# The temperature-threshold set-up ahead of the constants, and two places for the tail copies, in a fused attention and mixture-of-experts kernel

## The chip, the cores and the metric

The kernel runs on one core of a Trainium2 chip. Times are microseconds (us) of the device. A run of the program is one execution; three executions of the kernel before are timed, and one more was taken with the profiler, which gives the trace.

## The reference

The program computes attention with a threshold, and passes its result, token by token, to a mixture of experts with one chosen expert per token:

```python
scores = scale * np.matmul(q, k.transpose(0, 1, 3, 2))      # 4 batches, 8 heads, 576 x 576, head size 64
thresh = np.max(scores, axis=-1, keepdims=True) - tau
scores = np.where(scores >= thresh, scores, -1e9)
attn = softmax(scores); attn_out = attn @ v
x = attn_out.transpose(0, 2, 1, 3).reshape(2304, 512)
expert = argmax(x @ w_gate)                                  # 8 experts, 576 rows of capacity each
out[i] = gate_w[i] * (relu(x[i] @ w1[expert]) @ w2[expert])  # 512 -> 1024 -> 512
```

Everything is in 32-bit floating point; `tau` is one number that arrives in memory as an input.

## The kernel before, in words

**Staging.** The 32 (batch, head) combinations are worked as 16 pairs `s` of two heads; four pairs make a batch (`s` = 4b + a, a = 0 to 3). Per pair the kernel loads k, q and v; splits q and k into a high and a low 16-bit part ("hi" on ScalarE, `emit_hi` L767; "lo" on VectorE for the first two pairs and on GpSimd for the others, `emit_lo` L775); turns both so that the head size lies on partitions (`kT`, `qT`); makes the scores `s` on TensorE and their row maxima on VectorE (`emit_max`); works out each row's threshold (`emit_m`), which is added to q as two more columns and turned again ("tm"); makes the scores a second time, transposed and with the threshold in them (`d`); takes the exponential on ScalarE and masks on VectorE (`emit_keep` L940); splits the probabilities into two 16-bit parts; multiplies by v into the bank `xo` (`emit_av`); copies `xo` to `xs` on ScalarE (`emit_xe` L982), sums and inverts the denominators on VectorE (`emit_r`), and scales on GpSimd into the token rows `xr` (`emit_xm` L994).

**Tails.** 576 rows are four blocks of 128 and a tail of 64. The part x = 2 of a pair is the tail of both heads: 64 partitions, 2 x 64 columns. Pairs a = 0, 1 put it on partitions 0 to 63, pairs a = 2, 3 on partitions 64 to 127, in the tile `xrt`, which holds one batch's tails. All 16 pairs use one tile `xs2` for the copy and one for the reciprocals.

**The first pair** is turned differently: on TensorE, by a matmul with the identity (`emit_pturn` L804: k high, k low, then q), and copied out by VectorE and ScalarE (`emit_pturned` L809, `emit_hi_rows` L816). In the text below, hik0 and lok0 are the high and low part of k of pair 0, likewise hiq0, hik1 and so on; ptk0, ptk1 and ptq0 are the three matmul turns; pck0 and pck1 copy the turned k (VectorE and ScalarE), pcq0 and pcq1 the turned q (VectorE and ScalarE); vs0 and vh0 scale and round v of pair 0, vs1 that of pair 1. tq1, tk1 are the turns of pair 1, done by DMA from the SyncE queue. The score matmuls of pair 0 read kT and qT, so they need all four copies.

**Set-up.** Before the pairs VectorE fills constants (L264 to L293), clears the pad columns of `kn`, `qn`, `xs` (L732 to L740), and only then, in program order, does `emit_tau` (L295): the two numbers `g` (tau's sign, times 64) and `ntau`, from `tau_t`. `g` is the scale that hiq0 and hiq1 multiply with.

**The planner.** The order of everything after the set-up is worked out when the program is built, by a list scheduler (class `Plan`). Each piece of work is a task with an engine, a planned duration, tasks that it must follow, and a priority (lower goes first). Going forward in planned time, the planner gives an engine the task of lowest priority number among those that could start within 90 ns of the first one that could (`WINDOW`). For a task that follows a load, the earliest start is the planned end of the transfer plus `LAND[kind]`; all tasks that follow work on an engine get some 150 to 230 ns for the hand-over. The result is one fixed order per engine; on the chip each engine takes its instructions in that order, and a wait of the one at the head holds all that follow. The planner's times are nowhere on the chip; they only set the order.

The loads go out on SyncE (k0, then q1, then k1), ScalarE (q0) and GpSimd (v0, v1). After the pairs come the experts' matmuls (from about 333 us), whose code is the same before and after.

Of the kernel before, what the change touches and what calls it, by code (L numbers as in the profile page):

```python
# [10 lines left out]
F32 = mybir.dt.float32  # L11
# [4 lines left out]
ALU = mybir.AluOpType  # L16
# [4 lines left out]
P = 128  # L21
QK_SCALE = 64.0
# [4 lines left out]
MC = 4096.0  # L27
# [7 lines left out]
class Plan:  # L35
# [155 lines left out]
def attention_moe_kernel(ctx: ExitStack, tc: tile.TileContext, q, k, v, tau, w_gate, w1, w2, cap, out):  # L191
    nc = tc.nc
    B, H, S, D = q.shape
    NTOK, DM = out.shape
    E, _, F = w1.shape
    NJ = S // P
    TAIL = S - NJ * P
# [15 lines left out]
    const = ctx.enter_context(tc.tile_pool(name="const", bufs=1))  # L213
# [12 lines left out]
    V = nc.vector  # L226
# [11 lines left out]
    cum = const_of("cum", [E], F16)  # L238
# [45 lines left out]
    V.tensor_scalar(out=half[:, 0:1], in0=tok_l, scalar1=float(HP), scalar2=None, op0=ALU.is_ge)
    V.tensor_copy(out=hslot[:, 0:2], in_=hs_i)
    V.scalar_tensor_tensor(
        out=half[:, 1:2], in0=half[:, 0:1], scalar=-float(HP), in1=tok_l, op0=ALU.mult, op1=ALU.add
    )
    for t in (slice(0, NF), slice(NL, SLOTS)):
        V.tensor_scalar(out=hslot[:, 0, t], in0=hslot[:, 0, t], scalar1=half[:, 0:1], scalar2=None, op0=ALU.add)  # L290
    V.tensor_scalar(
        out=hslot[:, 2], in0=hslot[:, 0], scalar1=float(HP), scalar2=half[:, 1:2], op0=ALU.mult, op1=ALU.add
    )  # L293

# [374 lines left out]
    if True:  # L669
# [324 lines left out]
        def emit_xm(s, x):  # L994
            t, _, r1, rows, n = xs_of(s, x)
            b, a, _ = heads_of(s)
            if b not in xrows:
                xrows[b] = [xp.tile([P, NJ, ROW], F32, name="xr", tag="xr"), None]
            if x == 2 and xrows[b][1] is None:
                xrows[b][1] = xp1.tile([P, 1, HD], F32, name="xrt", tag="xrt")  # L1000
            if x < 2:
                h = 2 * a + x
                out = xrows[b][0][:, :, h * D + h // HH:h * D + h // HH + D]
            else:
                out = xrows[b][1][rows, 0, a % 2 * P:(a % 2 + 1) * P].rearrange("p (x d) -> p x d", d=D)
            nc.gpsimd.tensor_tensor(out=out, in0=t[:, :, 0:D], in1=r1.to_broadcast([P if x < 2 else TAIL, n, D]), op=ALU.mult)

# [217 lines left out]

        T("xd0", "S", 1150, first_row, [("s", 1, 4)], 20, dma=20, kind="rows")
        plan.fill = lambda *_: 0
        T(("ltau",), "S", 475, lambda: nc.sync.dma_start(out=tau_t, in_=tau.partition_broadcast(P)), [], -60, dma=60, kind="load")
# [5 lines left out]
        T(("lwg",), "S", 475, lambda: nc.sync.dma_start(out=wg[:, :, 0:E], in_=w_gate.rearrange("(c p) e -> p c e", p=P)), [("s", 1, 2)], 20, dma=230, kind="load")  # L1234

# [6 lines left out]
        for s in range(NPR):  # L1242
# [3 lines left out]
            for is_q in (False, True):  # L1246
                n = "q" if is_q else "k"
                src, raws = (q, qraws) if is_q else (k, kraws)
                eng, en, occ = (nc.scalar, "A", 460) if (s, is_q) in FIRST_A else (nc.sync, "S", 600)
                T(("l" + n, s), en, 3 * occ, partial(load, src, raws[s % NRAW], s, eng), last("lo" + n, s - NRAW) + ([("tk", 0), ("tq", 0)] if s == 2 else [("tk", 2), ("tq", 2)] if s == 3 else []), u + PR["ld"] + is_q, dma=(728, 90, 90), kind="load")  # L1250
                nat = s - (NQN if is_q else NKN)
# [11 lines left out]
                if s == 0:  # L1263
# [12 lines left out]
                    continue  # L1276
                T(("t" + n, s), "S", 0, partial(emit_turn_q if is_q else emit_turn_k, s), [("lo" + n, s)] + users + ([("tm", 0)] if s == 2 else []), u + PR["tk"] + is_q, dma=2016, kind="turn")
            vfree = last("av", s - NV, 2, 0) + last("av", s - NV, 1, NJ - 1)
# [43 lines left out]
            for x in range(3):  # L1322
# [298 lines left out]
```

## Time and profile before

| | us |
|---|---|
| three timed executions | 615.66, 617.41, 619.67 |
| their median | 617.41 |
| the profiled execution | 614.46 |
| its span, first to last instruction | 612.4 |
| time of the profiled execution outside the span | 2.06 |
| mean granted clock of TensorE | 0.967 of full speed |

Engines are named PE (TensorE), PEld (its weight loads), DVE (VectorE), ACT (ScalarE), POOL (GpSimd), SP (SyncE); a "q" behind the name is the engine's sequencer or its DMA queue. A start in a view is counted from the first instruction of the span. The stretch up to 16 us is the set-up with pair 0's turns; the score matmuls of pair 0 begin at about 14 to 15 us; attention ends at about 345 us.

### The profile page before, as it was taken

What the parts mean: (1) busy time and instruction counts of PE and PEld (TensorE: products, weight loads), DVE (VectorE), ACT (ScalarE), POOL (GpSimd) and SP (SyncE); (2) the same over time, 40 slices, a digit from 0 to 9 for tenths busy, and PEclk for the clock granted to TensorE, in tenths of its full rate; (3) what the DMA queues carried; (4) which work ended last, traced back from release to release, by engine and by line L of the source; (5) the groups of instructions that cost most, each with busy time, mean ns of one, the idle gap of its engine ahead of it and who ended that gap; (6) DMA issues with size and microseconds to landing.
All of it is one profiled execution on the core that took longest, in us unless ns stands there. A gap on an engine that the chain in (4) does not pass through costs nothing.

```text
span 612.4 us, 16304 instructions
## 1 busy us (share of the span) xinstructions
PE 529.5 (86%) x6122; PEld 343.0 (56%) x6122; DVE 433.5 (71%) x999; ACT 396.5 (65%) x551; POOL 446.6 (73%) x382
## 2 busy tenths in 40 slices
PE   2868889887998979997687868699999999999993
PEld 1334545554664646665466744575774687468651
DVE  5886787889897899887776895355555555555652
ACT  5585887897897869896378755356676547625400
POOL 5365967878997689897499446308998868956864
PEclk9897999999999999998798988899999999999997
DMA  6967775578777686872152868754497529643952
GB/s 142 167 123 152 137 155 106 130 105 190 123 151 138 103 205 117 139 106 70 60 155 91 294 190 256 201 65 138 172 232 201 167 84 266 193 169 78 209 179 102
DMA packets 165327, 92.80 MB, mean 152 GB/s; under 512 B 141172, under 2 KB 153528, under 8 KB 165243
## 3 DMA queue, kind: packets, MB, share of 16 engines
q1 hardware_dynamic: 152458, 49.59, 43.0%
q0 software_dynamic: 12352, 41.80, 21.1%
q8 instruction: 53, 0.87, 0.6%
q10 hardware_dynamic: 432, 0.30, 0.2%
q14 instruction: 32, 0.25, 0.1%
HBM read 53.25 MB, written 10.24 MB: 104 GB/s over the span
## 4 chain that ended last, share of the span: by engine, by line
PE 61%; DVE 13%; DMA 11%; ACT 6%; POOL 4%; issue 3%; another core or an unknown queue 1%; SPq 0%; POOLq 0%; ACTq 0%; DVEq 0%
PE b L406 12%; PE s L846 7%; DMA qT<-qn 6%; PE d L846 6%; PE b L399 6%; PE gp L445 6%; PE xo L445 6%; PE xo L958 6%; PE b L445 5%; DVE mx L873 3%; PE xo L970 3%; DMA out_dram<-latey,oix 2%; DVE w2b L942 2%; DVE w1b L942 2%; POOL p L912 2%
## 5 line engine op out<-in xcount | busy, mean ns | idle before, releaser
L873 DVE TENSOR_REDUCE mx<-s 128x1 f32<-128x512 f32 x144 | 95.4, 680 | 26.6 <-PE s L846 25.9
L846 PE MATMUL s<-kT,qT 128*128 128x512 f16 (+2 forms) x576 | 95.8, 306 | 21.1 <-DMA qT<-qn 8.3
L846 PE MATMUL d<-qT,kT 128*128 128x512 f16 (+2 forms) x576 | 88.5, 305 | 10.4 <-DVE w1b L942 4.2
L406 PE MATMUL b<-w1b,latex 128*128 (+2 forms) x816 | 80.7, 276 | 6.9 <-ACT latex L376 3.2
L331 ACT ACTIVATE ws<-ws 128x1024 f32<-128x1024 f32 x48 | 50.5, 1051 | 47.7 <-DMA ws<-in_moe_w_dram 47.7
L406 PEld LDWEIGHTS <-latex 128*128 128x128 f16 (+1 forms) x816 | 63.1, 103 | 23.2 <-issue 6.5
L942 DVE SCALAR_TENSOR_TENSOR w2b<-d,ntau,w2b 128x1024 f32<-128x1024 f32 x56 | 71.4, 1275 | 5.0 <-ACT w2b L938 4.7
L334 POOL TENSOR_TENSOR w1b<-ws,w1b 128x1024 f16<-128x1024 f32 x24 | 51.2, 2142 | 29.8 <-ACT w1b L332 29.6
L912 POOL TENSOR_TENSOR p<-w2b,p 128x1024 f16<-128x1024 f32 x33 | 70.5, 2144 | 2.6 <-DMA qr<-in_q_dram 1.5
L334 POOL TENSOR_TENSOR w2b<-ws,w2b 128x1024 f16<-128x1024 f32 x24 | 51.0, 2137 | 20.5 <-ACT w2b L332 20.3
L938 ACT ACTIVATE w2b<-d 128x1024 f32<-128x1024 f32 x56 | 57.1, 1019 | 12.5 <-PE d L846 12.2
L846 PEld LDWEIGHTS <-qT 128*128 128x128 f16 (+1 forms) x640 | 34.9, 102 | 53.7 <-issue 25.4
L846 PEld LDWEIGHTS <-kT 128*128 128x128 f16 (+1 forms) x640 | 36.6, 101 | 49.9 <-issue 31.1
L445 PEld LDWEIGHTS <-lateh 128*128 128x128 f16 (+1 forms) x408 | 30.7, 103 | 33.8 <-issue 0.8
L958 PEld LDWEIGHTS <-p 128*128 128x128 f16 x1056 | 41.9, 99 | 11.3 <-POOL p L912 1.8
L399 PEld LDWEIGHTS <-w1b 128*128 128x128 f16 x768 | 43.9, 98 | 6.9 <-issue 5.4
L399 PE MATMUL b<-earlyx,w1b 128*128 128x128 f16 x768 | 47.1, 219 | 0.0
L958 PE MATMUL xo<-vH,p 128*128 128x65 f16 x704 | 45.2, 196 | 1.7 <-POOL p L912 1.7
L958 PE MATMUL xo<-vL,p 128*128 128x64 f16 x352 | 41.9, 193 | 0.4 <-issue 0.4
L332 ACT ACTIVATE w2b<-ws 128x1024 f16<-128x1024 f32 x24 | 25.4, 1057 | 21.2 <-PE gp L445 20.6
L318 POOL DMA_DIRECT2D ws<-in_moe_w_dram x50 | 37.4, 751 | 1.2 <-POOL w2b L334 0.9
L908 ACT ACTIVATE p<-w2b 128x1024 f16<-128x1024 f32 x33 | 34.7, 1056 | 0.4 <-DVE w2b L942 0.4
(250 smaller groups left out, 1228.6 us busy)
## 6 DMA issues: line engine op xcount, KB each, us to landing
ws<-in_moe_w_dram POOLq DMA_DIRECT2D x50, 512.0 KB
ws<-in_moe_w_dram SPq DMA_DIRECT2D x14, 512.0 KB
kr<-in_k_dram SPq DMA_DIRECT2D x16, 256.0 KB
qr<-in_q_dram SPq DMA_DIRECT2D x15, 256.0 KB
v<-in_v_dram SPq DMA_DIRECT2D x28, 128.0 KB
kr<-in_k_dram SPq DMA_DIRECT2D x32, 16.0 KB
v<-in_v_dram POOLq DMA_DIRECT2D x4, 128.0 KB
qr<-in_q_dram SPq DMA_DIRECT2D x30, 16.0 KB
```

Source lines behind the costliest of these rows:

```text
L318: eng.dma_start(out=t, in_=src)
L331: nc.scalar.activation(out=t, in_=t, func=AF.Copy, scale=W_SCALE)
L334: nc.gpsimd.tensor_tensor(out=dst[:, :, 1, :], in0=t, in1=dst[:, :, 0, :], op=ALU.subtract)
L399: nc.tensor.matmul(out=hp[:, f * P:(f + 1) * P], lhsT=wb[0][:, o:o + P], rhs=xT[t][:, xi], start=(d == 0 and z == 0), stop=(d == NB - 1 an ...
L406: nc.tensor.matmul(out=hp[m, 0:FC], lhsT=xT[t][:, xi, m], rhs=wb[0][:, bass.ds(r + (2 * d + wi) * FC, FC)], start=(d == 0 and z == 0), sto ...
L445: nc.tensor.matmul(out=yp[m], lhsT=h[:, o, hi, m], rhs=wb[1][:, bass.ds(r + wi * DM, DM)], start=(z == 0), stop=(z == len(ops) - 1),)
L846: nc.tensor.matmul(out=out, lhsT=l, rhs=r, start=(z == 0), stop=(z == 1), **kw)
L873: V.tensor_reduce(out=m[:, i, 0:1], in_=ps_s[i % 2], axis=AX.X, op=ALU.max)
L912: eng.tensor_tensor(out=p[:, 1], in0=x, in1=p[:, 0], op=ALU.subtract)
L938: nc.scalar.activation(out=t, in_=d, func=AF.Exp, scale=sc_s)
L942: V.scalar_tensor_tensor(out=t, in0=d, scalar=ntau, in1=t, op0=ALU.is_ge, op1=ALU.mult)
L958: nc.tensor.matmul(out=ps_x[:, j * DV:j * DV + r.shape[-1]], lhsT=l, rhs=r, start=(z == 0), stop=(z == len(ops) - 1))
```

## The change

Three things are done.

1. `emit_tau` stands ahead of most of the set-up. On VectorE there remain before it `ones`, `ident16`, the pads of buffer 0 (`pads(0)`) and one memset of `qT`. The rest are tasks of the plan that follow tau on VectorE: `("pad", 1)` (planned 800 ns, priority -59), `("pad", 2)` (400 ns, -30), `("const", 0)` (1500 ns, -12) and `("const", 1)` (1000 ns, -11). Users of these constants get the tasks as predecessors.
2. The planner's landing times: tau's goes from 560 to 2100 ns (kind "tau"), that of k0 and q0 from 560 to 2300 ns (kind "load0"). All other loads, q1 and k1 among them, keep 560.
3. The tail copy has two tiles, `xs2` and `xs3` (by a % 2), of two blocks instead of four, and `emit_xe` of a tail follows the scaling of two pairs back, not of the pair before. In pairs a = 2, 3 the scaling of the tail runs over all 128 partitions: the 64 of this pair and again the 64 of pair a - 2, which lie in the same tile.

```diff
-    LAND = {"load": 560, "turn": 960, "rows": 2000, "move": 1030, "gather": 980}
+    LAND = {"load": 560, "tau": 2100, "load0": 2300, "turn": 960, "rows": 2000, "move": 1030, "gather": 980}
...
     V.memset(ones, 1.0)
-    V.memset(cum, 0.0)
-    V.memset(wg, 0.0)
-    V.memset(zero, 0.0)
...
+    def more_consts(i):
+        if i == 0:
+            V.memset(cum, 0.0)
+            V.memset(wg, 0.0)
+            V.memset(zero, 0.0)
+            for i in range(2):
+                V.tensor_copy(out=tri2[:, i * HP:(i + 1) * HP], in_=tri[:, 0:HP])
...
+            return
+        V.tensor_copy(out=hslot[:, 0:2], in_=hs_i)
...
-        xss = [right.tile([P, NJ, D + 2], F32, name=f"xs{i}") for i in range(3)]
-        rcs = [right.tile([P, 2, NJ, 1], F32, name=f"rc{i}") for i in range(3)]
+        xss = [right.tile([P, NJ if i < 2 else 2, D + 2], F32, name=f"xs{i}") for i in range(4)]
+        rcs = [right.tile([P, 2, NJ, 1], F32, name=f"rc{i}") for i in range(4)]
...
+        def pads(i):
+            if i < NKN:
+                V.memset(kns[i][:, 1, :, D:], 0.0)
+                V.memset(kns[i][:, 1, :, D:D + 1], MC)
+                V.memset(kns[i][:, 1, :, D + 1:D + 2], 1.0)
+            V.memset(qns[i][:, 1, :, D:], 0.0)
+
+        def small_pads():
+            for t in xss:
+                V.memset(t[:, :, D + 1:], 1e-9 * QK_SCALE)
+
+        pads(0)
         V.memset(qTs[0][D:, 1], 0.0)
...
         def xs_of(s, x):
-            i = (3 * s + x) % 3
+            i = x if x < 2 else 2 + s % HH % 2
...
             else:
+                if a >= HH // 2:
+                    i, rows = 2 + a % 2, slice(0, P)
+                    t, r1 = xss[i][:, 0:2], rcs[i][:, 1, 0:2]
                 out = xrows[b][1][rows, 0, a % 2 * P:(a % 2 + 1) * P].rearrange("p (x d) -> p x d", d=D)
-            nc.gpsimd.tensor_tensor(out=out, in0=t[:, :, 0:D], in1=r1.to_broadcast([P if x < 2 else TAIL, n, D]), op=ALU.mult)
+            m = P if x < 2 or a >= HH // 2 else TAIL
+            nc.gpsimd.tensor_tensor(out=out, in0=t[:, :, 0:D], in1=r1.to_broadcast([m, n, D]), op=ALU.mult)
...
-        T(("ltau",), "S", 475, ..., [], -60, dma=60, kind="load")
+        T(("ltau",), "S", 475, ..., [], -60, dma=60, kind="tau")
         T(("tau",), "V", 140, emit_tau, [("ltau",)], -60)
+        T(("pad", 1), "V", 800, lambda: pads(1), [("tau",)], -59)
+        T(("pad", 2), "V", 400, lambda: (pads(2), small_pads()), [("tau",)], -30)
+        T(("const", 0), "V", 1500, lambda: more_consts(0), [("tau",)], -12)
+        T(("const", 1), "V", 1000, lambda: more_consts(1), [("const", 0)], -11)
...
-                T(("l" + n, s), en, 3 * occ, ..., dma=(728, 90, 90), kind="load")
+                T(("l" + n, s), en, 3 * occ, ..., dma=(728, 90, 90), kind="load" if s else "load0")
...
-                T(("xe", s, x), "A", 370 if x < 2 else 240, ..., [("av", s, x, j) for j in js] + last("xm", s - 1, x), ...)
+                T(("xe", s, x), "A", 370 if x < 2 else 240, ..., [("pad", 2)] + [("av", s, x, j) for j in js] + last("xm", s - (1 if x < 2 else 2), x), ...)
```

## Rows read from the trace of the kernel before

**Rows 1.** The page, part 1: busy us, share of the span and instructions of each engine.
```profile
PE 529.5 (86%) x6122; PEld 343.0 (56%) x6122; DVE 433.5 (71%) x999; ACT 396.5 (65%) x551; POOL 446.6 (73%) x382
```

**Rows 2.** The chain of waits that ended last, up to 16 us: start, length, what.
```profile
7.21 3.96 DMA kr<-in_k_dram
...
12.47 0.76 DVE kn L782
13.23 0.68 DVE qT L814
...
15.11 0.40 PE s L846
```

**Rows 3.** The timeline of DVE from the start: start, length, instruction, [idle before, releaser].
```profile
3.27 0.17 DVE L285 CAST hslot<-w2b 128x46 f32<-128x46 int32 x1
...
4.12 0.30 DVE L733 MEMSET kn<- 128x288 uint32 x1
...
6.78 0.15 DVE L296 TENSOR_SCALAR g<-tau_t 128x1 f32<-128x1 f32 x1
```

**Rows 4.** The timeline of ACT from the start.
```profile
6.96 1.25 ACT L773 ACTIVATE qn<-qr,g 128x1152 f16<-128x1152 f32 x1 [4.65 <-DVE g L296]
8.12 1.15 ACT L773 ACTIVATE kn<-kr 128x1152 f16<-128x1152 f32 x1
9.18 1.24 ACT L773 ACTIVATE qn<-qr,g 128x1152 f16<-128x1152 f32 x1
10.32 0.72 ACT L788 ACTIVATE v<-v 128x640 f32<-128x640 f32 x1
11.28 1.16 ACT L773 ACTIVATE kn<-kr 128x1152 f16<-128x1152 f32 x1 [0.23 <-DMA kr<-in_k_dram]
12.35 1.11 ACT L812 ACTIVATE kT<-d 128x1152 f16<-128x1152 f16 x1
13.93 1.12 ACT L817 ACTIVATE qT<-d 64x1152 f16<-64x1152 f16 x1 [0.47 <-DVE qT L814]
14.96 0.73 ACT L791 ACTIVATE vH<-v 128x650 f16<-128x650 f32 x1
```

**Rows 5.** The timeline of PE from the start.
```profile
9.32 2.10 PE L807 MATMUL d<-ident,kn 128*128 128x128 f16 x18 [9.32 <-ACT kn L773]
11.31 1.03 PE L807 MATMUL d<-ident,qn 128*128 128x128 f16 x9
```

**Rows 6.** The waits of SP's queue: total us, times, longest; first 100 us.
```profile
SPq L761 <- DMA tau_t<-in_tau_dram: 0.3, 1, 0.3
```

**Rows 7.** The timeline of SP's queue: issue of each transfer.
```profile
4.07 1.94 SPq L761 DMA_DIRECT2D qr<-in_q_dram  x2
...
12.01 3.39 SPq L833 DMA_TRANSPOSE qT<-qn  x1
...
40.15 1.40 SPq L761 DMA_DIRECT2D kr<-in_k_dram  x2
41.66 1.35 SPq L838 DMA_TRANSPOSE qT<-qn  x1
```

**Rows 8.** ACT's queue (q0's load), 5.5 to 6 us: packets, MB, share of 16 engines.
```profile
q10 hardware_dynamic: 3, 0.00, 0.6%
```

**Rows 9.** SP's queue of DMA, 10 to 11 us, in the same columns.
```profile
q1 hardware_dynamic: 20, 0.00, 2.0%
```

**Rows 10.** The scaling of L1006 by shape: duration ns min/median/max; and its last waiter.
```profile
L1006 POOL TENSOR_TENSOR xr<-xs,rc x32: 602/615/977, 47.5 to 343.4; 128x256 f32<-128x256 f32 x32
L1006 POOL TENSOR_TENSOR xrt<-xs,rc x16: 389/399/422, 66.9 to 349.0; 64x128 f32<-64x128 f32 x16
...
  PE gp L1011: 3.6, 2
```

**Rows 11.** The chain of waits that ended last, 36 to 60 us.
```profile
37.85 0.19 DVE qn L892
...
41.66 4.87 DMA qT<-qn
```

More of the change, by code (lines that the diff above doesn't have):

```diff
@@ L284, in attention_moe_kernel @@
[L284 to L293, printed above, removed]
+    def more_consts(i):
[5 more added lines that the diff above has]
+                V.tensor_copy(out=tri2[:, i * HP:(i + 1) * HP], in_=tri[:, 0:HP])
+            V.tensor_copy(out=desc, in_=desc_i)
+            V.tensor_copy(out=tok_f, in_=tok_i)
+            V.tensor_copy(out=tok_l, in_=tokl_i)
+            V.tensor_scalar(
+                out=row_e, in0=desc, scalar1=-float(NTOK), scalar2=float(E * NTOK), op0=ALU.mult, op1=ALU.add
+            )
+            V.tensor_scalar(
+                out=more_e, in0=desc, scalar1=float(E - NP), scalar2=float(HP), op0=ALU.is_gt, op1=ALU.mult
+            )
+            V.tensor_scalar(out=half[:, 0:1], in0=tok_l, scalar1=float(HP), scalar2=None, op0=ALU.is_ge)
+            return
+        V.tensor_copy(out=hslot[:, 0:2], in_=hs_i)
+        V.scalar_tensor_tensor(
+            out=half[:, 1:2], in0=half[:, 0:1], scalar=-float(HP), in1=tok_l, op0=ALU.mult, op1=ALU.add
+        )
+        for t in (slice(0, NF), slice(NL, SLOTS)):
+            V.tensor_scalar(out=hslot[:, 0, t], in0=hslot[:, 0, t], scalar1=half[:, 0:1], scalar2=None, op0=ALU.add)
+        V.tensor_scalar(
+            out=hslot[:, 2], in0=hslot[:, 0], scalar1=float(HP), scalar2=half[:, 1:2], op0=ALU.mult, op1=ALU.add
+        )
@@ L1224, in first_row @@
                 )
-        T("xd0", "S", 1150, first_row, [("s", 1, 4)], 20, dma=20, kind="rows")
+        T("xd0", "S", 1150, first_row, [("s", 1, 4), ("const", 0)], 20, dma=20, kind="rows")
         plan.fill = lambda *_: 0
-        T(("ltau",), "S", 475, lambda: nc.sync.dma_start(out=tau_t, in_=tau.partition_broadcast(P)), [], -60, dma=60, kind="load")
+        T(("ltau",), "S", 475, lambda: nc.sync.dma_start(out=tau_t, in_=tau.partition_broadcast(P)), [], -60, dma=60, kind="tau")
         T(("tau",), "V", 140, emit_tau, [("ltau",)], -60)
+        T(("pad", 1), "V", 800, lambda: pads(1), [("tau",)], -59)
+        T(("pad", 2), "V", 400, lambda: (pads(2), small_pads()), [("tau",)], -30)
+        T(("const", 0), "V", 1500, lambda: more_consts(0), [("tau",)], -12)
+        T(("const", 1), "V", 1000, lambda: more_consts(1), [("const", 0)], -11)
         T(("lcap",), "S", 475, lambda: nc.sync.dma_start(out=cap_i, in_=cap.partition_broadcast(P)), [("s", 1, 3)], 20, dma=60, kind="load")
@@ L1233, in attention_moe_kernel @@
             out=pick, in_=view(ident[:, 0:E], [[1, E], [P // NB, NB]]), axis=AX.X, op=ALU.add), [("tau",)], 25)
-        T(("lwg",), "S", 475, lambda: nc.sync.dma_start(out=wg[:, :, 0:E], in_=w_gate.rearrange("(c p) e -> p c e", p=P)), [("s", 1, 2)], 20, dma=230, kind="load")
+        T(("lwg",), "S", 475, lambda: nc.sync.dma_start(out=wg[:, :, 0:E], in_=w_gate.rearrange("(c p) e -> p c e", p=P)), [("s", 1, 2), ("const", 1)], 20, dma=230, kind="load")
         CUT = 2 * NJ + 3
@@ L1249, in attention_moe_kernel @@
                 eng, en, occ = (nc.scalar, "A", 460) if (s, is_q) in FIRST_A else (nc.sync, "S", 600)
-                T(("l" + n, s), en, 3 * occ, partial(load, src, raws[s % NRAW], s, eng), last("lo" + n, s - NRAW) + ([("tk", 0), ("tq", 0)] if s == 2 else [("tk", 2), ("tq", 2)] if s == 3 else []), u + PR["ld"] + is_q, dma=(728, 90, 90), kind="load")
+                T(("l" + n, s), en, 3 * occ, partial(load, src, raws[s % NRAW], s, eng), last("lo" + n, s - NRAW) + ([("tk", 0), ("tq", 0)] if s == 2 else [("tk", 2), ("tq", 2)] if s == 3 else []), u + PR["ld"] + is_q, dma=(728, 90, 90), kind="load" if s else "load0")
                 nat = s - (NQN if is_q else NKN)
@@ L1276, in attention_moe_kernel @@
                     continue
[L1277 removed]
+                T(("t" + n, s), "S", 0, partial(emit_turn_q if is_q else emit_turn_k, s), [("lo" + n, s), ("pad", min(s, 2))] + users + ([("tm", 0)] if s == 2 else []), u + PR["tk"] + is_q, dma=2016, kind="turn")
             vfree = last("av", s - NV, 2, 0) + last("av", s - NV, 1, NJ - 1)
@@ L1331, in attention_moe_kernel @@
                 t1 = t0 + PR["avj"] * len(js)
-                T(("xe", s, x), "A", 370 if x < 2 else 240, partial(emit_xe, s, x), [("av", s, x, j) for j in js] + last("xm", s - 1, x), t1 + PR["xe"], kind="psum")
+                T(("xe", s, x), "A", 370 if x < 2 else 240, partial(emit_xe, s, x), [("pad", 2)] + [("av", s, x, j) for j in js] + last("xm", s - (1 if x < 2 else 2), x), t1 + PR["xe"], kind="psum")
                 T(("r", s, x), "V", 200, partial(emit_r, s, x), [("xe", s, x)], t1 + PR["xe"])
```

19 lines of the change are left out of this document (removed).

## The prediction

> **What bounds the kernel now.** I read the page's first part, then the chain of waits, then the timelines of the engines up to 16 us, where the change works. No engine is at its limit over the whole span: TensorE is busy 86% of it, VectorE 71%, GpSimd 73% [rows 1]. While attention runs, the pairs follow one another through orders that are fixed, and a delay of the first pair has nothing behind it that is known to give it back; so I ask what sets the start of the first pair's scores. The chain shows it: the last piece of k1 lands at 7.21 + 3.96 = 11.17; hik1 runs on ScalarE at once (11.28, 1.16 long); lok1 on VectorE follows (12.47), then pcq0 (13.23), then pcq1 on ScalarE (13.93, 1.12 long), and the scores that need it start at 15.11 [rows 2, 4]. It is pair 1's k, not pair 0's data and not tau, that holds pair 0, since hik1 and lok1 stand ahead of pair 0's last copies in their queues.
>
> Tau is late too: hiq0 starts at 6.96 after 4.65 us of idle, released by `g` at 6.78, at the end of VectorE's set-up [rows 3, 4]. Tau itself was there by 4.07: SP's queue waited 0.3 us for it in front of that issue [rows 6, 7].
>
> **Step 1, tau ahead of the constants.** VectorE then has `ones`, `ident16`, one buffer's pads and the `qT` memset before `emit_tau`, and is done with them before 4.07; `g` is out at about 4.3. hiq0 now waits for q0. ACT's DMA queue still moves 3 packets of it between 5.5 and 6 [rows 8], and hiq0 found it landed at 6.96, so it lands between 5.5 and 6.96; I take 6.0, next to the packets. Gain for hiq0: about 1.0 us (0 to 1.5). The memsets and constants that move behind tau fill VectorE from 4.3 to about 6.5, when it would wait for hiq0 anyway: cost nothing. If that cover were gone, const1, the only part that falls later, costs 0.85 (3.27 to 4.12 [rows 3]) before pck0.
>
> **Step 2, the order that the planner now writes.** This decides. I worked the planner's rule by hand with its own constants (planned ns, which set the order and no time). Done that way for the kernel before, it gives ScalarE hiq0, hik0, hiq1, vs0, hik1, pck1, pcq1, vh0, vs1, and that is what rows 4 show. With the new landing times:
> - k0's transfer ends at 4354, so hik0 may start at 4354 + 2300 = 6654 (before 4914). q1's ends at 5352 and keeps 560: 5912. So hiq1 goes ahead of hik0: hiq0 4203, hiq1 5912, hik0 7082, hik1 (7420) 8252 to 9422.
> - VectorE: const0 at 5372 (loq0, ready at 5555, is outside the 90 ns), loq0, loq1, lok0 (8434 to 9194), const1 (9194), pck0, lok1, pcq0.
> - ptk1 then ends at 10456, so pck1 may start at 10683; at 9422 vs0 is ready, at 10332 vh0, and both go before pck1 (11022). At 12272 vs1 (ready 12503) goes before pcq1 (12850). The margins on ScalarE are 347 ns and more, beyond the window; the one near tie is lok0, 42 ns after const1 could start at 8392 and so inside it.
>
> New order on ScalarE: hiq0, hiq1, hik0, hik1, vs0, vh0, pck1, vs1, pcq1. Three instructions of the v path, two for v0 and one for v1, now stand between hik1 and pcq1.
>
> On the chip: hiq1 waits for q1, whose last piece is issued in the stretch 4.07 to 6.01 [rows 7] and had landed by hiq1's start at 9.18 [rows 4]: between 6.01 and 9.18, I take 8.0, toward the later end, since k1's last piece took 3.96. hik0 then ends near 10.4 (11.6 at the late end), and hik1 still starts at 11.28 to 11.6, because k1's load is untouched. From there ScalarE has 1.16 + 0.72 + 0.73 + 1.11 + 0.72 + 1.12 = 5.56 us to the end of pcq1 [rows 4], vs1 priced as vs0: 16.84. Starts overlap a little (hik1 to pck1 1.07 for 1.16), about 0.09 at four hand-overs: 16.5. Before, pcq1 ended at 15.05. So the scores of pair 0 start 1.4 to 1.8 later; I take **1.5 us**. VectorE doesn't set it: at the late end lok0 ends at 12.4, const1 at 13.2, pck0 at 14.0, ptq0 (1.03 [rows 5]) at 15.0, pcq0 (0.75 at most) at 15.8, about when ScalarE comes to pcq1. What is queued behind pcq1 (vh1, then pair 2's k) and SP's loads of pair 2, which wait for all four copies, shift with it.
>
> **Step 3, turns of pair 1.** tq1 was issued at 12.01 [rows 7]; loq1 now ends near 10, so tq1 goes out near 10, and tk1 near 13.5, before pair 2's loads. Pair 1's scores wait for pair 0's maxima, so no gain. k1 is still in flight at 10: SP's DMA queue moves 20 packets between 10 and 11 [rows 9]. I take 0 for the collision; at most hik1 is late by the issue of one turn, 1.35 to 3.39 [rows 7]. The Trainium skill (DMA: Bandwidth & Descriptors, "Issuing engines are not separate DMA queues") says that all transfers interleave on the same 16 engines, which speaks against moving a turn up into a load. By it k1 is delayed; by the rows the 20 packets are 2.0% of the engines' time there, so little is left to delay.
>
> **Step 4, tails.** 8 of 16 tail scalings (pairs a = 2, 3) go from 64 to 128 partitions. The trace has 399 ns for 64x128 and 615 for 128x256; 128x128 lies between, so 0 to 8 x 0.216 = 1.7 us on GpSimd, spread over 300 us of an engine that is 73% busy: 0 on the path. I take 0.40 for one, as the columns are the same; if GpSimd's slack were gone, the 1.7 would show. The Trainium skill (GPSIMD Engine Reference, "Architecture") says that each of eight cores works on its own 16 partitions, which makes the length that of one core's share: by it 0.40, by the upper row 0.62; no run here shows 128x128. The second place removes a wait of the tail copy on the scaling a pair before; the scaling's waiters in the trace are TensorE's turns alone, the last 3.6 us in two [rows 10], no ScalarE copy. Gain 0.
>
> **Sum.** +1.5 on the profiled execution: 614.46 + 1.5 = 616.0. That execution is 3.0 under the median of the three timed ones; the mean of all four is 616.8. I forecast **618.3**, no change that can be told: about 1% (6 us) is what a measurement of this kernel tells from none.
>
> **Rivals.**
> - *The start gains, as if pair 0's copies came first.* If hik0 follows hiq0 and pcq0, pcq1 pass hik1: hiq0 6.0 to 7.2, hik0 to 8.4, lok0 9.2, ptk0 10.2, pck0 11.0, ptq0 12.0, pcq0 12.8, pcq1 13.9; 1.1 us before 15.05, up to 2.1 with q0 at 5.5 and overlaps: 614.7 to 615.7. For it: hiq0's 4.65 us of idle. Against: the planned order above. 0.17.
> - *The start doesn't move*: the order stays and k1's landing at 11.17 pins it: 616.8. 0.12.
> - *Faster by a shuffle of SP's queue.* The threshold of pair 1 is done at 37.85 + 0.19 = 38.04, but its turn goes out at 41.66, behind loads that fill SP's queue until 41.55, and TensorE gets it 4.87 later [rows 7, 11]. A planner started from other times can put that turn ahead: 3.6 us from one such place, more from two: 613.2 to 609.6 from 616.8. For: any new input reshuffles such ties. Against: nearly all later tasks shift together. 0.14.
> - *Slower than before by over 1%, the same place turned round.* One more load's last pieces ahead of the turn in SP's queue cost 1.40 to 1.94 [rows 7]. For: SP's queue has no gap before 41.66. Against: the loads shift along with the turns. At one pair in four it costs 4 x 1.94 = 7.8: 618.3 + 7.8 = 626.1. It decides from three pairs on (624.1). 0.11.
> - *Forecast*: 0.46.
>
> **Range and chances.** From the gain of one shuffle with the early start (616.8 - 3.6 - 1.1 = 612.1) to the forecast with two lost loads (618.3 + 3.9 = 622.2), with a little for the timed runs, which differ by 4.0 among themselves: 611.8 to 622.6. Faster by over 1% (under 611.2): the shuffle's two-place end, 0.10. Slower by over 1% (above 623.6): nearly all of that rival, 0.10. Within: the rest, 0.80.
>
> **What would show it.** After: `g` near 4.3, hiq0 near 6; hiq1 before hik0; vs0, vh0 and vs1 before pcq1; pcq1's end near 16.5; the 128x128 scaling near 0.40 us. Wrong if hik0 is ScalarE's second, if pcq1 ends before 15, or if a shift of more than 2 us appears between 40 and 340 us.

## The result, and the profile after

The changed kernel took 620.86 us (median of 13 executions, 615.17 to 626.32), the kernel before on the same chip 616.05 (median of 13). The ratio is 1.0065, 95% interval 1.0041 to 1.0089: 4.0 us slower, a small loss that is clear of the noise, and under the 1% that I called a change. The medians take in every execution; the ratios and their intervals leave out the few slow ones. The profiled execution took 621.26 us, with a span of 619.2 (612.4 before) and a mean granted clock of 0.961 (0.967 before). Of a span 6.8 us longer, part belongs to that one execution, so the runs decide and the profile only says where.

The page, part 1 (against [rows 1]): the engines do the same work.

```profile
PE 533.0 (86%) x6122; PEld 348.4 (56%) x6122; DVE 436.5 (70%) x1000; ACT 397.0 (64%) x551; POOL 445.5 (72%) x382
```

The chain of waits that ended last, up to 17 us (start, length, what), against [rows 2]: k1 still opens it in this execution (by a wait of 0.22 us; see step 2 below), and the v path (`v`, `vH`) now lies in it.

```profile
7.31 3.62 DMA kr<-in_k_dram
...
12.11 0.73 ACT v L794
...
15.25 1.02 ACT qT L823
...
16.31 0.40 PE s L852
```

VectorE's timeline, the row that answers to the last of [rows 3]: `g` is out at 4.09 instead of 6.78.

```profile
4.09 0.15 DVE L298 TENSOR_SCALAR g<-tau_t 128x1 f32<-128x1 f32 x1 [0.95 <-DMA tau_t<-in_tau_dram]
```

ScalarE's timeline, against [rows 4]: hiq0, hiq1, hik0, hik1, vs0, vh0, pck1, vs1, pcq1, the order that was forecast. pcq1 ends at 16.26 instead of 15.05. In the first row the view names `more_e`, a constant that hiq0 does not read, because it ended last; in runs 2, 9, 11 and 12 below, with the same start, the view names q0's load, and hiq0 starts at 6.19 to 6.28. The last row, pair 2's first scaling of k, turned out to matter more; before, it began at 19.55.

```profile
6.25 1.25 ACT L779 ACTIVATE qn<-qr,g 128x1152 f16<-128x1152 f32 x1 [3.94 <-DVE more_e L282]
8.51 1.25 ACT L779 ACTIVATE qn<-qr,g 128x1152 f16<-128x1152 f32 x1 [1.01 <-DMA qr<-in_q_dram]
9.67 1.15 ACT L779 ACTIVATE kn<-kr 128x1152 f16<-128x1152 f32 x1
11.04 1.16 ACT L779 ACTIVATE kn<-kr 128x1152 f16<-128x1152 f32 x1 [0.22 <-DMA kr<-in_k_dram]
12.11 0.72 ACT L794 ACTIVATE v<-v 128x640 f32<-128x640 f32 x1
12.86 0.75 ACT L797 ACTIVATE vH<-v 128x650 f16<-128x650 f32 x1
13.51 1.11 ACT L818 ACTIVATE kT<-d 128x1152 f16<-128x1152 f16 x1
14.52 0.73 ACT L794 ACTIVATE v<-v 128x640 f32<-128x640 f32 x1
15.15 1.11 ACT L823 ACTIVATE qT<-d 64x1152 f16<-64x1152 f16 x1
...
21.32 0.68 ACT L771 ACTIVATE kr<-kr 128x576 f32<-128x576 f32 x1 [4.43 <-DMA kr<-in_k_dram]
```

SP's queue, against [rows 7]: q's turn of pair 1 (tq1), k's (tk1), then pair 2's load of k (lk2). Before, lk2 was issued at 15.46 and tk1 behind pair 2's loads, at 19.09. Before, then after:

```profile
15.46 0.57 SPq L758 DMA_DIRECT2D kr<-in_k_dram  x1
...
19.09 2.76 SPq L828 DMA_TRANSPOSE kT<-kn  x1
```

```profile
10.64 2.86 SPq L839 DMA_TRANSPOSE qT<-qn  x1
13.73 3.34 SPq L834 DMA_TRANSPOSE kT<-kn  x1
17.12 0.58 SPq L764 DMA_DIRECT2D kr<-in_k_dram  x1
```

The scaling on GpSimd by shape (mean ns behind the busy time), against [rows 10]: the new 128x128 form takes as long as 64x128.

```profile
L1016 POOL TENSOR_TENSOR xrt<-xs,rc 128x128 f32<-128x128 f32 x8 | 3.2, 399 | 0.0
L1016 POOL TENSOR_TENSOR xrt<-xs,rc 64x128 f32<-64x128 f32 x8 | 3.2, 397 | 0.0
```

Where the time appears. ScalarE's copies of a finished tail (`xs<-xo 64x130`, one per pair) serve as milestones. Against before they start 1.6 earlier in pair 0, 0.0 in pair 1 (84.30), then 1.6 later in pair 2, 2.4 in pair 7, 3.8 in pair 9 and 3.9 in pair 14; the last head copy, at 346.79, is 6.6 late. The experts' matmuls behind add nothing. Pair 2's copy, before and after:

```profile
103.52 0.27 ACT L985 ACTIVATE xs<-xo 64x130 f32<-64x130 f32 x1
```

```profile
105.09 0.27 ACT L991 ACTIVATE xs<-xo 64x130 f32<-64x130 f32 x1
```

The step between pairs 1 and 2 lies in a stretch where TensorE's clock was partly at the lower of its two levels (1.2 and 2.4 GHz); before, it was not. The view gives busy time by stretch, then the granted clock; first before, then after:

```profile
90.00:100.00 10.00, 7.45 (x100) 4.87 (x100) 6.70 (x18) 5.89 (x8) 6.75 (x7) 1.00 0.40 86
...
330.00:340.00 10.00, 9.28 (x178) 8.83 (x177) 7.64 (x15) 7.71 (x16) 9.08 (x7) 0.85 0.45 137
```

```profile
90.00:100.00 10.00, 7.63 (x93) 5.09 (x94) 4.38 (x12) 4.72 (x8) 5.49 (x5) 0.83 0.28 62
...
330.00:340.00 10.00, 7.76 (x97) 7.29 (x98) 5.71 (x9) 6.24 (x12) 9.63 (x7) 0.66 0.07 24
```

TensorE is as busy at 90 to 100 and gets less done, 93 matmuls instead of 100. But such falls lie elsewhere in before: from 45 to 55 us its clock was 0.63 and 0.69, where after has 1.00 (and 0.66 from 40 to 45). Take for each stretch of 5 us its length times what its clock was short of 1, and add up to 340 us: 11.9 us in both profiles. So the clock does not by itself explain what after has lost by then.

### The profile page after: what moved, and what is told of

The parts are those of the page before. It is cut to its first block, busy times and chain, and to the rows that moved or that the text cites. A ratio compares the mean times of both kernels' runs of the same rounds, so it can differ in the third digit from the quotient of the medians.

```text
span 619.2 us, 16310 instructions
## 1 busy us (share of the span) xinstructions
PE 533.0 (86%) x6122; PEld 348.4 (56%) x6122; DVE 436.5 (70%) x1000; ACT 397.0 (64%) x551; POOL 445.5 (72%) x382
## 4 chain that ended last, share of the span: by engine, by line
PE 57%; DVE 13%; DMA 13%; ACT 6%; POOL 6%; issue 5%; another core or an unknown queue 1%; SPq 0%; POOLq 0%; ACTq 0%; DVEq 0%
PE b L408 11%; DMA qT<-qn 8%; PE s L852 7%; PE b L401 7%; PE d L852 6%; PE xo L964 6%; PE gp L447 4%; PE xo L447 4%; PE b L447 4%; PE xo L976 3%; DVE mx L879 3%; DMA out_dram<-latey,oix 2%; DVE w2b L948 2%; PE b L375 2%; POOL p L918 2%
## 5 line engine op out<-in xcount | busy, mean ns | idle before, releaser
L852 PE MATMUL s<-kT,qT 128*128 128x512 f16 (+2 forms) x576 | 95.1, 304 | 25.3 <-DMA qT<-qn 14.2
L852 PE MATMUL d<-qT,kT 128*128 128x512 f16 (+2 forms) x576 | 86.1, 301 | 7.9 <-DVE w1b L948 5.2
L408 PE MATMUL b<-w1b,latex 128*128 (+2 forms) x816 | 82.6, 280 | 5.5 <-ACT latex L378 5.1
L964 PEld LDWEIGHTS <-p 128*128 128x128 f16 x1056 | 43.2, 101 | 13.2 <-issue 3.4
L964 PE MATMUL xo<-vH,p 128*128 128x65 f16 x704 | 46.7, 198 | 2.1 <-POOL p L918 2.1
```

The lines of the kernel that those rows point to most:

```text
L408: nc.tensor.matmul(out=hp[m, 0:FC], lhsT=xT[t][:, xi, m], rhs=wb[0][:, bass.ds(r + (2 * d + wi) * FC, FC)], start=(d == 0 and z == 0), sto ...
L852: nc.tensor.matmul(out=out, lhsT=l, rhs=r, start=(z == 0), stop=(z == 1), **kw)
L964: nc.tensor.matmul(out=ps_x[:, j * DV:j * DV + r.shape[-1]], lhsT=l, rhs=r, start=(z == 0), stop=(z == len(ops) - 1))
```

## The experiments

Three chips were used (runs 1 to 4, 5 to 8, 9 to 12), on which the kernel before took 615.54, 604.12 and 603.45 us (medians), so only ratios are compared. The ratio given is not the quotient of the two medians. In nine of the thirteen rows the two lie within 0.3% of each other. In run 1 the quotient is 1.0007 (615.97 by 615.54), in run 3 1.0101 (621.74), in run 7 1.0003 (604.29 by 604.12), in run 11 1.0059 (607.04 by 603.45), and I cannot say why; so what rests on run 1 or run 7 alone is weak.

The places in the last columns are weaker still. Before has one kept profile, so runs 5 to 12 are set against another chip; most of the difference between the chips lies behind attention (from the last head copy to the end of the span 272.2 us in before, 262.9 to 267.0 in runs 5 to 12), but how much lies in it is not known. Runs 7 and 12 are one and the same kernel on two chips: their tail copies agree within 0.3 us in pair 2 and differ by 1.3 in pair 7 and 3.1 in pair 14. The columns: ratio to before on the same chip; from the one profiled execution, by how much the tail copies of pairs 2 and 7 start later than before's (103.52 and 197.20), and the sum of TensorE's waits from 30 to 350 us that a turn (kT or qT) ended. Before has 13.1 us of these.

| kernel | ratio (95%) | pair 2, pair 7 | waits for turns |
|---|---|---|---|
| after | 1.0065 (1.0041 to 1.0089) | +1.6, +2.4 | 14.2 |
| 1 tails alone | 1.0051 (1.0018 to 1.0084) | -0.5, 0.0 | 12.9 |
| 2 new start, old order | 1.0006 (0.9973 to 1.0039) | -1.9, -1.4 | 12.2 |
| 3 old start, new order | 1.0145 (1.0112 to 1.0178) | +2.7, +2.8 | 14.7 |
| 4 pair 0 delayed | 1.0083 (1.0052 to 1.0114) | +2.5, +3.0 | 11.0 |
| 5 after, tk1 back | 1.0084 (1.0053 to 1.0116) | +3.2, +3.7 | 17.2 |
| 6 before, tk1 ahead | 1.0029 (0.9998 to 1.0061) | +2.3, +1.7 | 11.4 |
| 7 loads first | 0.9964 (0.9930 to 0.9999) | -1.3, +0.2 | 11.5 |
| 8 after, old tails | 1.0060 (1.0030 to 1.0091) | +4.4, +3.9 | 15.1 |
| 9 after, old queue | 1.0046 (1.0020 to 1.0072) | 0.0, +0.8 | 14.2 |
| 10 before, new queue | 1.0050 (1.0023 to 1.0077) | +3.3, +4.9 | 13.5 |
| 11 loads first, new tails | 1.0028 (0.9998 to 1.0059) | 0.0, +0.5 | 13.2 |
| 12 loads first, again | 0.9982 (0.9957 to 1.0008) | -1.1, -1.1 | 11.8 |

### 1. The tails alone

Before with part 3 and nothing else; the planned order is that of before.

```diff
-            i = (3 * s + x) % 3
+            i = x if x < 2 else 2 + s % HH % 2
...
+                if a >= HH // 2:
+                    i, rows = 2 + a % 2, slice(0, P)
```

> The kernel before with the third part of the change alone: two places for the tail copies, and pairs a = 2, 3 scale 128 partitions; set-up, landing times and the order on every engine as before. Theory 1 (the loss comes from the start and what follows from it): no change, within 1.5 us of 616. Rival (the tails cost what the start doesn't explain): about 2 us or more slower, and the 128x128 scaling clearly above 0.40 us or a new wait in front of a tail copy.

Median 615.97, ratio 1.0051. Neither sign of the rival came: the 128x128 scaling took 399 ns, and no tail copy waited for a scaling. One place can be read exactly. The first scatter of a batch's rows on GpSimd goes out 0.5 us later behind the same releaser, the scaling of `xr` behind it as well, and TensorE's turn of `xr` waits 1.25 us instead of 0.74. Before, GpSimd then TensorE:

```profile
213.70 1.03 POOL L1157 DMA_INDIRECT xd<-xr,ixi  x1 [1.86 <-DVE ixi L1151]
```

```profile
217.98 0.44 PE L1011 MATMUL gp<-ident,xr 128*128 128x128 f32 x2 [0.74 <-issue]
```

The tails alone, the same two:

```profile
214.23 1.03 POOL L1161 DMA_INDIRECT xd<-xr,ixi  x1 [2.37 <-DVE ixi L1155]
```

```profile
218.52 0.44 PE L1015 MATMUL gp<-ident,xr 128*128 128x128 f32 x2 [1.25 <-issue]
```

The fourteen profiles agree: the nine with old tails show 1.86 or 1.87 us of idle there and 0.74 or 0.75 on TensorE, the five with new tails 2.37 and 1.24 or 1.25; in the second batch it is 2.94 to 2.97 against 3.44 to 3.46. The instruction lists name a difference at this place, a second wait of the scatter, on GpSimd's own semaphore (before, then the tails alone):

```
102 L1157 DMA xd<-xr,ixi 18432x514 [waits DVE_49]
102 L1161 DMA xd<-xr,ixi 18432x514 [waits DVE_49,Pool_49]
```

In the trace it shows as semaphore instructions of GpSimd's sequencer at the scatter's line, 1 before and 12 with the tails alone (count and duration in ns):

```profile
L1157 POOLq EVENT_SEMAPHORE  x1: 17/17/17, 358.4 to 358.4; - x1
```

```profile
L1161 POOLq EVENT_SEMAPHORE  x12: 17/17/9789, 137.2 to 363.4; - x12
```

In the old form the tail's scaling carried that wait. That the second wait is what takes the 0.5 us fits in all of them, but was not tried by itself. Two such places make 1.0 us of the 3.1 that the ratio asks (0.0051 x 615.5); the rest was not found.

### 2. The new start with the old order

After's set-up, landing times and start up to pair 0's copies; behind it, and on SP's queue, the order that the planner writes for before; old tails.

```diff
-        plan.run()
...
+        plan.emit(plan.schedule(plan.tasks), plan.schedule(before))   # start tasks of the first, the rest of the second
```

> The first two parts of the change, for the start alone: set-up and the order of pair 0 and 1's preparation as in the changed kernel, everything behind it in the order of the kernel before, tails as before. Theory 1 (a later start is passed on whole): pcq1 ends near 16.3 instead of 15.05, and the time is 1.2 to 1.5 us above 616. Rival (the reordered work of pairs 1 to 5 loses the time, the start is absorbed): less than 0.7 above. Rival (all of the loss is in the start): about 4 above.

1.0006. Pair 0's scores start 1.7 us later than before (16.83 against 15.11), and yet the tail copies come 1.6 earlier in pair 0 and 1.4 to 1.9 in pairs 2 to 7: the late start is not passed on. Pair 2's k is scaled at 17.98, 1.6 earlier than before. The interval (0.9973 to 1.0039) is 2 us to either side and would not by itself exclude 1.5; the places do. TensorE, then the SyncE queue, where tq1 goes out earlier (11.35) and draws lk2 along:

```profile
16.83 0.82 PE L853 MATMUL s<-kT,qT 128*128 128x512 f16 x3 [0.77 <-ACT qT L824]
```

```profile
11.35 2.79 SPq L840 DMA_TRANSPOSE qT<-qn  x1
14.25 0.51 SPq L765 DMA_DIRECT2D kr<-in_k_dram  x1
```

### 3. The old start with the new order

Before's set-up and start, and behind it the order that the planner writes for after; old tails.

```diff
-        plan.run()
...
+        plan.emit(plan.schedule(plan.tasks), plan.schedule(after))
```

> The kernel before, with its set-up, its start and its tails, but everything behind the start in the changed kernel's planned order (it differs for pairs 0 to 6 only). Theory 1: 0.5 to 1 us above 616, since the milestones of the two traces move apart by 0.7 more between pair 0 and pair 5. Rival (the order loses most of the 4 us): 2.5 or more above. Rival (the order is neutral): within 0.4 us, with the whole loss in the start.

1.0145, the slowest of all, although pair 0's scores start at 14.93, 0.2 us sooner than before. So the order behind the start loses time by itself. On SP's queue tk1 stands ahead of pair 2's load, as in after:

```profile
15.06 2.70 SPq L829 DMA_TRANSPOSE kT<-kn  x1
17.82 0.58 SPq L759 DMA_DIRECT2D kr<-in_k_dram  x1
```

### 4. Pair 0 delayed

Before with eight more copies on ScalarE ahead of pcq1, 6.17 us of work.

```diff
         def emit_hi_rows(s, i):
+            for _ in range(8):
+                nc.scalar.activation(out=vHs[2], in_=vts[0], func=AF.Copy)
```

> The kernel before with eight more copies on ScalarE right ahead of pcq1 (each reads v of pair 0 and writes a buffer that is not in use yet, 0.6 to 0.7 us apiece), order and planned order unchanged: a pure delay of pair 0's scores by about 5 us, four times that of the change. Theory 1 (no slack behind the start): 5 us above 616, the milestones of every pair 5 us later. Rival (the pipeline absorbs a late start): 2 us or less above, with the milestones closing up over the first pairs.

1.0083, or 5.1 us, which is what theory 1 asked for. The places do not bear theory 1 out. The scores of pair 0 start 5.1 us late (20.25), but the tail copies of pairs 0 and 1 only 1.2 and 1.1. The copies also hold ScalarE, which comes to pair 2's k at 22.14, 2.6 late, and the milestones settle at +2.5 to +3.0 up to pair 7; the last head copy is 2.9 late. The profiled execution, the slowest of the seven, loses 7 us more behind it (279.4 us from there to the end, 272.2 in before), which the edit does not touch. The run shows that a late pair 0 is largely absorbed by pair 0's tail; it does not separate that delay from the one of pair 2, and its time is not explained.

```profile
20.25 5.99 PE L848 MATMUL s<-kT,qT 128*128 128x512 f16 x13 [6.25 <-ACT qT L819]
```

### 5 and 6. One turn on SP's queue

Four readings so far (2, 3, 4 and after) agreed that the milestones follow pair 2's k, and in 3 and after that one is late because tk1 was put ahead. My theory then was that this one move is the cause. Run 5 is after with tk1 put back behind pair 2's loads, run 6 is before with tk1 put ahead of them:

```diff
-        for start, _, k in sorted(order):
+        order = sorted(order)
+        turn = next(o for o in order if o[2] == ("tk", 1))
+        order.remove(turn)
+        order.insert([o[2] for o in order].index(("lq", 2)) + 1, turn)   # 6: index(("lk", 2))
+        for start, _, k in order:
```

> The kernel after with one thing undone: k's turn of pair 1 (tk1) is issued behind pair 2's loads of k and q (lk2, lq2) on SP's queue, as it was before; start, order of the other engines and tails stay those of after. Theory (SP's queue order of pair 2's loads sets the pace, the late start of pair 0's scores is absorbed): lk2 issued near 13.6 instead of 17.12, first scaling of pair 2's k near 18.0 instead of 21.32, the tail copies of pairs 2 to 7 at -1.5 to -2.0 against before instead of +1.6 to +2.4, time within 1.5 us of before (1.000 to 1.003, the upper part if the tails cost what the tails alone seemed to, 0.5%). Rival 1 (pair 0's scores, 1.2 us late, are passed on whole): milestones stay at +1.2 to +1.5 and the time near that of after, 1.004 to 1.008. Rival 2 (it is the rest of the planner's new order): milestones near +2.4, 1.006 to 1.010.

> The kernel before with one thing done: k's turn of pair 1 is issued ahead of pair 2's loads of k and q on SP's queue, as in after; all else as before. Theory (SP's queue order): pair 2's k is asked for near 18 instead of 15.46, its first scaling near 22.0 instead of 19.55, tail copies of pairs 2 to 7 at +2.4 to +2.8, time 1.004 to 1.010. Rival (pair 0's delay is the cause): pair 0's scores are not moved, milestones within 0.5 of before, 0.998 to 1.002. Rival (the turn done 4 us sooner lets pair 1's scores start sooner, a gain): milestones below -0.5, under 0.998.

Run 6 moved pair 2 as the theory said: pair 2's k is scaled at 22.11 instead of 19.55, and its tail copy comes 2.3 late. The time did not come out: 1.0029, between the theory (from 1.004) and its rival (to 1.002), with an interval that does not exclude no change, and the copies of pairs 4 to 11 are only 1.0 to 2.2 late, those of pairs 12 to 14 early. Before, then run 6, on ScalarE:

```profile
19.55 0.68 ACT L765 ACTIVATE kr<-kr 128x576 f32<-128x576 f32 x1 [2.46 <-DMA kr<-in_k_dram]
```

```profile
22.11 0.68 ACT L769 ACTIVATE kr<-kr 128x576 f32<-128x576 f32 x1 [5.35 <-DMA kr<-in_k_dram]
```

Run 5 refuted it as the sole cause: pair 2's k is scaled at 17.14, the tail copy of pair 0 comes 2.6 early, and yet the kernel is at 1.0084, with the tail copy of pair 2 3.2 late. TensorE, no longer held by pair 2's k, waited longer for the turns of q, at 56, 73 and 94 us (3.62, 2.58, 3.39 us), and behind each of them its clock fell (0.67 from 55 to 60, and the stretches below):

```profile
73.46 0.78 PE L856 MATMUL s<-kT,qT 128*128 128x512 f16 x2 [2.58 <-DMA qT<-qn]
94.02 0.85 PE L856 MATMUL s<-kT,qT 128*128 128x512 f16 x2 [3.39 <-DMA qT<-qn]
```

```profile
70.00:80.00 10.00, 7.42 (x93) 5.25 (x92) 5.73 (x14) 5.73 (x7) 5.35 (x5) 0.83 0.56 107
90.00:100.00 10.00, 6.61 (x77) 3.92 (x76) 4.95 (x16) 5.36 (x7) 6.62 (x6) 0.83 0.48 97
```

A longer wait alone does not decide it. In run 2 TensorE waited 2.54 us at 90.65 and stayed at 1.00; in run 7, after 2.51 us at 89.64, the clock granted from 90 to 95 was 0.66 (in run 12, the same kernel, 0.71).

### 8. After with the old tails

```diff
-            i = x if x < 2 else 2 + s % HH % 2
+            i = (3 * s + x) % 3
...
```

> The kernel after without part 3: one place for the tail copy, the tails scaled on 64 partitions for every pair; start and order of after. If part 3 costs 0.5% (the reading of the tails alone): time 1.5 to 3 us under after, 1.001 to 1.004 of before, most of the difference behind 215 us. If it costs nothing, as the prediction had it: 1.005 to 1.009 of before and milestones of after within 0.4 up to 320 us. If two places give a gain that the tails alone could not show: over 1.009.

1.0060 against 1.0065 for after on another chip: behind the new order the tails show no cost, though the 0.5 us on TensorE is gone (0.74). Start and new order without the tails are thus enough for the result. By the two intervals a cost of 0.3% would not show, and the milestones missed: they were to lie within 0.4 us of after's and come 2.8 later in pair 2.

### 9 and 10. SP's whole queue against the other engines' order

Run 9 keeps every engine's order of after and puts SP's queue wholly in the order of before; run 10 does the opposite. Engines other than SP have the same instruction lists as after and before.

```diff
-        plan.run()
...
+        loads = [k for k in plan.schedule(before) if plan.tasks.get(k, " ")[0] == "S"]   # 10: schedule(after)
+        plan.emit(plan.tasks, loads)   # the plan's order, but SP's tasks among themselves as in loads
```

> The kernel after, every engine's order as in after (start and tails included), but SP's whole queue in the order of before: pair 2's loads ahead of k's turn of pair 1, and later tq4 ahead of tk4 and the loads of pair 4's v behind those of k. Putting k's turn of pair 1 back alone left the time at 1.008. Theory A (the whole new order of SP's queue, not that one turn, makes it slower): near before, 0.999 to 1.003, PE's wait ahead of pair 4's scores near 1.7 us instead of 2.4 to 2.6. Theory B (the new order of TensorE, VectorE, ScalarE and GpSimd over pairs 0 to 6 makes it slower: PE comes to the scores of pairs 2, 4 and 5 earlier or with less other work behind, waits longer there, and its clock falls): 1.005 to 1.009, whatever the queue.

> The kernel before, every engine's order and the start as in before, but SP's whole queue in the order of after. Theory A (SP's queue makes it slower): 1.005 to 1.010. Theory B (the order of the other engines): 0.999 to 1.004, no more than the one moved turn gave by itself (1.003).

Run 10: 1.0050. The queue's order alone costs what theory A asked, at its lower end; the interval (1.0023 to 1.0077) reaches into B's range. The new queue has not only tk1 ahead: pair 4's k is turned before its q, so that q's turn goes out at 69.02 instead of 64.97. That swap does not show as a cost: the scores of pair 4 wait 1.92 us for q's turn, and before 1.77 for k's. Three stretches lose clock that did not before (1.00 in all three):

```profile
70.00:80.00 10.00, 8.09 (x105) 5.26 (x102) 6.50 (x15) 6.29 (x8) 6.74 (x6) 0.83 0.69 120
90.00:100.00 10.00, 7.23 (x90) 4.39 (x87) 6.20 (x16) 5.53 (x8) 7.38 (x6) 0.83 0.71 113
150.00:160.00 10.00, 7.40 (x83) 4.51 (x83) 8.06 (x20) 8.11 (x10) 9.98 (x10) 0.85 0.71 119
```

Whether the order does that is not shown, since two executions of one kernel, here on two chips, can differ so. Run 7, then run 12:

```profile
150.00:155.00 5.00, 3.29 (x47) 2.38 (x46) 3.67 (x11) 4.00 (x5) 5.00 (x5) 0.72 0.78 150
```

```profile
150.00:155.00 5.00, 3.82 (x70) 2.65 (x68) 4.44 (x14) 4.43 (x6) 5.00 (x5) 1.00 0.68 143
```

Run 9: 1.0046, between the theories, with an interval (1.0020 to 1.0072) that touches both. Theory A's sign failed: TensorE waited 2.58 us ahead of pair 4's scores (2.44 in after), not near 1.7. Neither theory stands as the only cause: with the old queue most of the loss is still there, and with the new queue alone most of it is there too. If the new tails in run 9 cost the half per cent that runs 1 and 11 give them, nothing is left for the start and the engines' order; run 8, in which the tails cost nothing behind that order, speaks against it.

### 7, 11 and 12. Pair 2's loads first

Run 2 with pair 2's loads as early as their buffers allow, ahead of tq1; 11 is the same with the new tails, 12 the same again.

```diff
+        for k, behind in ((("lq", 2), ("loq", 0)), (("lk", 2), ("lok", 0)), (("tq", 1), ("lk", 2))):
+            order.remove(k)
+            order.insert(order.index(behind) + 1, k)
```

> After's start with before's order behind it and the old tails (as in the kernel with the new start alone), and on SP's queue pair 2's loads of k and q are issued as soon as their buffers are free, ahead of q's turn of pair 1: lq2 near 8.6, lk2 near 11.6, then tq1 near 13, tk1 near 16. Theory (pair 2's k and q set the pace): first scaling of pair 2's k near 16.8 instead of 17.98, tail copies of pairs 2 to 7 at -2.4 to -3.2 against before; time 0.994 to 0.998, or 0.998 to 1.002 if what is won ahead of 200 us is lost at the end of attention, as it was with the new start alone. Rival (pair 1's turns, now 2 to 3 us later, become the bound): pair 1's scores wait for tq1 and tk1, the milestones lie at -1.4 or above, 1.000 to 1.006.

> After's start, before's order behind it, pair 2's loads as early as their buffers are free (the kernel with the loads first), and the two places and the scaling on all partitions for the tails, all parts of the change but the planner's own new order. If part 3 costs something by itself: 0.3% or more over the same kernel with the old tails beside it in these runs; if not, within 0.2% of it and under 1.000 of before.

> The kernel with the loads first once more, unchanged, beside the same with new tails. If the gain over before is real: 0.993 to 0.999; if it was this kernel's luck on one chip: 0.999 to 1.003.

0.9964 and 0.9982: faster than after in both (the upper ends, 0.9999 and 1.0008, lie under after's 1.0041). A gain over before is not shown: only the first interval excludes none, and there the medians are equal (604.29 and 604.12). The scaling of pair 2's k came at 16.95, as expected, but the milestones at -1.3 and -1.1 in pair 2, where the rival had them and not the theory (-2.4 to -3.2). SP's queue in run 7:

```profile
8.38 0.37 SPq L769 DMA_DIRECT2D qr<-in_q_dram  x1
...
11.88 0.37 SPq L769 DMA_DIRECT2D kr<-in_k_dram  x1
...
13.46 3.20 SPq L844 DMA_TRANSPOSE qT<-qn  x1
16.77 2.72 SPq L839 DMA_TRANSPOSE kT<-kn  x1
```

Run 11 is 0.46% above run 12 beside it (1.0028 against 0.9982; by the medians, 607.04 and 602.66, 0.7%): with run 1 the second time that the new tails cost about half a per cent on the order of before, and the firmer one.

## Why the prediction was right, and where it was wrong

The time, the range and "no change over 1%" held. The order and the times up to 16 us held nearly as well; what follows from them did not, and that the sum came close is luck: a term that was too large stood for two that were missing.

- **Step 1, right.** `g` 4.09 (4.3 forecast), hiq0 6.25 (6.0); the constants behind tau cost nothing there.
- **Step 2, the order right, its consequence wrong.** The nine tasks on ScalarE came in the order that was worked out, pcq1 ended at 16.26 (16.5), the scores started 1.2 us later (1.5 taken, 1.4 to 1.8 stated). What holds them was wrong: not k1's load, whose landing was to set hik1's start, but q1's. In all eight profiles with the new start hiq1 waits for q1 (0.8 to 2.1 us) and starts between 8.34 and 9.59, and the scores start 7.6 to 7.8 us behind it, between 16.05 and 17.29; in six of them hik1 follows hik0 without a wait for k1. Then "nothing behind it that is known to give it back" failed: run 2 starts the scores 1.7 late at 1.0006, run 4 loses 5.1 at the start and 1.2 by pair 0's tail. The sentence that SP's loads of pair 2 wait for all four copies was wrong too: that is the planner's dependence, which sets the order. In run 4 lk2 was issued at 15.12, before pcq1 began (19.09). The term was +1.5; by the places of run 2 it is about 0.
- **Step 3, the times right, the price of the move wrong.** tq1 10.64 (near 10), tk1 13.73 (13.5), hik1 at 11.04. From the Trainium skill (DMA: Bandwidth & Descriptors, "Issuing engines are not separate DMA queues"), by which the transfers interleave, I had taken a delay of k1; the trace of after shows none but hardly tests it, since k1's last piece landed at 7.31 + 3.62 = 10.93, 0.3 us behind tq1's issue. What I left at 0 was the queue that the turn is moved past: lk2 behind it went from 15.46 to 17.12 and pair 2's k from 19.55 to 21.32. The queue's new order by itself is worth 0.50% (run 10: 0.0050 x 603.45, 3.0 us, by the interval 1.4 to 4.6); this one turn by itself gave 0.29%, which the noise does not tell from none (run 6).
- **Step 4, the size right, "0 on the path" wrong.** 128x128 took 399 ns (0.40 taken), as the Trainium skill's rule of 16 partitions to a core has it (GPSIMD Engine Reference, "Architecture"). No ScalarE copy gained. But the scatter lost 0.5 us, which TensorE waits for; on the order of before part 3 costs about 0.5% (run 11 beside 12, and run 1 by its ratio), behind the new order nothing that shows (run 8).
- **The sum.** 0 for the start, +3.0 for SP's queue and 0 to 3 for the tails, against +4.0 measured (0.0065 x 616). The parts don't add up to a sharper figure: start and order without the tails gave 1.0060, the order behind the old start 1.0145, and taking the queue's order (run 9) or the tails (run 8) out of after did not bring the time back. The queue's order is thus shown to be enough for most of the loss, not to be its only cause.
- **The rivals.** The one that was slower by over 1% named the right place, SP's queue without a gap, but with the wrong piece: not one more load ahead of the turns at several pairs, but a turn ahead of the loads at pair 1, where it makes pair 2's k 2.6 us late (run 6). "Faster by a shuffle" did not come with the planner's new order, and run 7, a shuffle by hand, shows no sure gain.
- **My own test.** "A shift of more than 2 us between 40 and 340 us" was to mean wrong; it was there (+2.4 by pair 7, +3.9 by pair 14).

**Open:** why the new order costs 1.45% behind the old start and 0.60% behind its own (by the medians 1.0% and 0.75%, so part of it may be noise); and whether the 2.7 us that after lost between 330 and 347 us belong to the change. From 330 to 340 us the clock was 0.66 also in runs 3, 4 and 10, of which run 4 has neither the new order nor the new tails, 0.83 in run 5, 0.87 to 0.90 in runs 1 and 2. How much of each loss is the wait and how much the clock that falls behind it was not separated: what the clock was short of 1 up to 340 us, added up as above, comes to 15.3 us in run 10 but 10.2 in run 8, and to 15.3 and 11.9 in runs 7 and 12, one kernel on two chips.

## What to carry to other kernels

Ask of a delay at the start which later instruction first waits for it, and of a step that is moved, who stood in the queue that it is moved past; here the second cost about 3 us (run 10) and the first nothing that shows (run 2). A dependence that stands only in the planner sets an order and is no wait on the chip. Where an instruction loses a wait because its buffer was doubled, look which later instruction inherits it: a scatter that had to wait for two things instead of one went out 0.5 us later.

## What the runs showed of the hardware

- Time goes with TensorE's mean granted clock from run to run of one kernel: over the 22 executions of before that the ratios of runs 1 to 4 use (611.7 to 618.8 us, clock 0.956 to 0.973) a straight line gives -3.6 us for +0.01, with a correlation of -0.84; on the two other chips -2.5 and -2.7 (-0.63 and -0.62). A stretch of 10 us at 0.83 lowers the mean of a span of 612 us by 10 x 0.17 / 612 = 0.0028; by these lines that goes with 0.7 to 1.0 us. This is an estimate from a correlation, and no run here shows that the clock is the cause.
- A tiny VectorE operation took 17 times as long in one run as in another. The same 64x8 sum took 2.37 us in run 12, up to 218.92, where GpSimd ran a scaling from 216.19 to 216.82 and behind it a 128x1024 multiply from 216.76 to 218.90, and 0.14 us in run 11, where it started 0.7 us before that multiply (218.88). The Trainium skill (SBUF — State Buffer, "SBUF: two separate sides") has a VectorE operation with two SBUF inputs and a GpSimd one that reads SBUF take turns at a port pair that is held for a whole instruction; that the sum and the multiply end within 0.02 us of each other agrees with that. Run 12, then run 11:

```profile
216.55 2.37 DVE L1133 TENSOR_TENSOR cum<-cum,oh 64x8 f16<-64x8 f16 x1
```

```profile
218.17 0.14 DVE L1137 TENSOR_TENSOR cum<-cum,oh 64x8 f16<-64x8 f16 x1
```
